# A gated linear attention kernel: state update products with 48 stationary columns in place of 64

## The chip, the cores and the metric

The kernel runs on one core of a Trainium2 chip. The metric is the device time of one execution in microseconds (us). The kernel before was timed in three runs. The trace and its page come from one further execution, taken by the hardware profiler.

The core has five engines that run their own instruction streams and wait for each other through semaphores: TensorE (matrix products, PE in the profile, with its weight loads listed apart as PEld), VectorE (DVE), ScalarE (ACT), GpSimd (POOL) and SyncE (SP), which issues the DMA transfers here. A product on TensorE has two steps: a *stationary* operand is loaded into the array (a weight load), and then a *moving* operand is streamed through it (the matmul). The result goes to PSUM, from where DVE and ACT read it.

## The reference

Two blocks follow each other. The first is a gated recurrence for 4 batches x 8 heads, 768 tokens and 48 channels per head; the second is a feed-forward block of 384 -> 2048 -> 384 with hardswish between. All is float32.

```python
state = np.zeros((B, H, D, D))                       # D = 48
for t in range(S):                                   # S = 768
    state = alpha[:, :, t, :, None] * state + np.einsum('bhd,bhe->bhde', k[:, :, t], v[:, :, t])
    y[:, :, t] = np.einsum('bhd,bhde->bhe', q[:, :, t], state)
x = y.transpose(0, 2, 1, 3).reshape(B * S, H * D)    # 3072 x 384
h = x @ w_in
out = (h * np.clip(h + 3.0, 0.0, 6.0) / 6.0) @ w_out
```

## The kernel before, in words

**The recurrence, by chunks.** The 3072 tokens are cut into 24 chunks of 128 tokens (six in each batch), and each chunk into two halves of 64. Heads go in pairs: head `a` (0 or 1) of pair `p` (0 to 3) has its 48 channels on the partitions `64*a` to `64*a + 47` of a 128-partition tile, and the 16 partitions behind them belong to no channel. A scan over the decays gives `R` (L309), and the keys are multiplied by it (L332), so that they stand in the scale of the chunk's end. The scaled keys are needed twice: by channel for the scores (L346), and by token as `kb`, for the state. For the first chunks `kb` is made by transposes on TensorE (L374) and an ACT copy (L378), for the later ones by way of a DRAM tile (`kw`, `kr`).

**The state.** For each chunk, `update` (L423 to L432; the products stand on L429) computes one 48 x 48 matrix per head and half: the half's 64 keys, by token, are the stationary operand, and the half's 64 rows of `v` are the moving one. With 4 pairs, 2 heads and 2 halves that makes 16 products, or 8 in the last chunk of a batch, where only the first half is wanted: 20 x 16 + 4 x 8 = 352 products in all. Each float32 product appears in the trace as two weight loads and two matmuls, so L429 has 704 of each. Each product uses one quarter of the array, a tile of 64 rows by 64 columns: the half `b` sets the rows, the head `a` the columns. The results lie in two PSUM banks, one for each half.

**Who uses it.** `next_state` (L435 to L440) adds these results to the state on DVE, over all 128 partitions and 192 columns at once: after the first half into `half_st` (L439 or, at a batch's start, L437), after the second into `sm`. `decayed_state` (L409, POOL) makes the next chunk's `st` of `sm`. `place_state` (L419, ACT) copies the state into rows of `v` for the product that makes the output `y` (`attend`, L455), and takes the 48 real rows of each head alone: `st[64 * a : 64 * a + D]`.

**The feed-forward block.** After the first chunks, which use plain products (L478, L489, L516), the two big products run on groups of 256 tokens with sums of blocks in place of some products (L600 for the first, L703 for the second). DVE makes the sums (L537 to L541, L647, L664), applies the hardswish (L498) and adds products; ACT copies PSUM banks out (L606) and does the first step of the hardswish (L494).

**The order.** The order of all instructions is written out by hand, as a list of words (`run(...)`, L751 to L900). `u.6.3.0` is `update` for chunk 6 with the PSUM banks 3 and 0. Each engine takes its instructions in that order, and waits on semaphores where an operand or a buffer isn't ready. No scheduler changes it.

Of the kernel before, what the change touches and what calls it, by code (L numbers as in the profile page):

```python
# [17 lines left out]
def kernel(  # L18
# [32 lines left out]
    nc = tc.nc  # L51
    B, H, S, D = q.shape
# [26 lines left out]
    half = consts.tile([C, 1], FP, tag="half")  # L79
# [141 lines left out]
    R_t, P_t, Q_t, K_t, kb_t, A_t, xT_t, ps_t = ({} for _ in range(8))  # L221
# [200 lines left out]
    def update(j, *at):  # L422
        for b, i in enumerate(at):  # L423
            ps_t["u", j, b] = banks[i][:, 0 : NP * D].rearrange("r (p n) -> r p n", p=NP)
        for p in range(NP):
            for a in range(2):
                for b in range(len(at)):
                    half = slice(HB * b, HB * b + HB)
                    nc.tensor.matmul(ps_t["u", j, b][64 * a : 64 * a + 64, p],  # L429
                                     kb_t[j][half, p, 64 * a : 64 * a + 64],  # L430
                                     v_t[j][half, b, 2 * p + a, 0:D],
                                     start=True, stop=True)  # L432

# [189 lines left out]
    def hidden1(g, o):  # L623
# [16 lines left out]
    b = {(i, k): w2[:, i * HF : (i + 1) * HF, k * HD : (k + 1) * HD]  # L640
         for i in range(2) for k in range(2)}
# [79 lines left out]
    def store2(g, i):  # L721
# [13 lines left out]
        "sc": scores, "m": masked, "qa": place_q, "kb": k_by_token, "ck": keep_k,  # L735
        "st": decayed_state, "sv": place_state, "kt": turn_k, "kw": write_k, "kr": read_k,
        "u": update, "sm": next_state, "ya": lambda j, i: attend(j, 0, i),
        "yb": lambda j: attend(j, 1), "cy": keep_x,
        "f": ff1, "fa": lambda i, m: ff1_half(0, i, m), "fb": lambda i: ff1_half(1, i, None), "fr": gate, "fg": hidden, "b": ff2, "bo": keep_out, "so": store, "x": combine_w2,
# [193 lines left out]
```

## Time and profile before

| what | value |
|---|---|
| median of 3 runs | 535.48 us (535.39 to 535.66) |
| the profiled execution: span, first to last instruction | 533.7 us |
| median less span | 1.8 us |
| granted TensorE clock over the span | 1.000 |
| PE busy / weight loads busy | 524.6 us (98%) / 499.4 us (94%) |
| DVE busy | 477.2 us (89%) |
| ACT busy / POOL busy | 257.2 us (48%) / 50.4 us (9%) |
| L429 matmuls, busy (704) | 16.8 us |
| L429 weight loads, busy (704) | 14.2 us |

The page gives the span of the profiled execution, and no total beside it; the 1.8 us by which the runs' median stands above the span is what lies around it. Busy time is a union: instructions of one engine that overlap are counted once, which is why 704 matmuls of 220 ns make only 16.8 us. In a line of groups, the shape `64*64` is rows x columns of the stationary operand, `64x48` is rows x columns of the moving one; after the bar come the busy time of the group in us and the mean length of one in ns, and then the time that the engine stood idle just before, with what ended it. The end of a matmul is modelled by the profiler, so that distances between starts say more than lengths.

### The profile page before, as it was taken

The page shows a single profiled execution, that of the slowest core. Times are in us where ns is not written, and L with a number is a line of the kernel's source. Part 1 is how long each engine was busy: PE and PEld are TensorE (multiplying, and loading weights), DVE is VectorE, ACT ScalarE, POOL GpSimd, SP SyncE. Part 2 cuts the span into 40 slices and gives each one's busy share as a digit, 9 for nine tenths or more (in the row PEclk, how much of TensorE's full clock was granted, in tenths as well). Part 3 has the DMA queues.
Part 4 walks back from the last instruction along what each step waited for, and adds up shares of the span by engine and source line. Part 5 has one row for each costly group of instructions (what it writes and reads, how often), then busy time and mean ns, then how long its engine had stood idle before and what let it go on. Part 6 is the DMA issues. An engine that isn't in the chain of part 4 may idle for free.

```text
span 533.7 us, 15143 instructions
## 1 busy us (share of the span) xinstructions
PE 524.6 (98%) x6306; PEld 499.4 (94%) x6306; DVE 477.2 (89%) x849; ACT 257.2 (48%) x503; POOL 50.4 (9%) x71
## 2 busy tenths in 40 slices
PE   8799999999999999999999999999999999999997
PEld 7698886789999999999999999999999999999997
DVE  6999989999999999998999999999999899496382
ACT  3889865212653553553544444642634544553340
POOL 5333425100000000000000000000000000000000
DMA  9998876005615155254344355044454042100001
GB/s 174 217 252 256 215 216 152 21 2 154 152 30 116 32 121 135 57 140 95 87 110 113 91 124 140 19 120 102 115 136 104 11 110 43 44 2 2 15 16 37
DMA packets 124100, 54.40 MB, mean 102 GB/s; under 512 B 83328, under 2 KB 116864, under 8 KB 124032
## 3 DMA queue, kind: packets, MB, share of 16 engines
q1 hardware_dynamic: 124032, 53.44, 42.5%
q8 instruction: 49, 0.80, 0.6%
q14 instruction: 19, 0.16, 0.1%
HBM read 44.50 MB, written 8.91 MB: 100 GB/s over the span
## 4 chain that ended last, share of the span: by engine, by line
PE 85%; DVE 8%; POOL 2%; DMA 2%; ACT 1%; issue 1%; SPq 1%; DVEq 0%; POOLq 0%
PE m_ps L703 34%; PE m_ps L600 34%; PE m_ps L478 5%; PE t_ps L455 4%; PE t_ps L346 2%; PE t_ps L429 2%; PE m_ps L489 2%; PE t_ps L282 1%; DVE rings L647 1%; DMA v<-in_v_dram 1%; DVE raw L537 1%; ACT raw L191 1%; DMA kq<-in_k_dram 1%; DVE g_sb L647 1%; DVE w L537 1%
## 5 line engine op out<-in xcount | busy, mean ns | idle before, releaser
L606 ACT COPY g_sb<-m_ps 128x512 f32<-128x512 f32 x110 | 63.6, 584 | 124.9 <-PE m_ps L600 104.1
L703 PE MATMUL m_ps<-w,g_sb 128*128 128x192 f32 x704 | 121.7, 327 | 0.0
L703 PEld LDWEIGHTS m_ps<-w,g_sb 128*128 128x128 f32 x704 | 113.7, 190 | 0.4
L703 PE MATMUL m_ps<-rings,g_sb 128*128 128x192 f32 x528 | 91.5, 326 | 0.0
L703 PEld LDWEIGHTS m_ps<-rings,g_sb 128*128 128x128 f32 x528 | 85.4, 190 | 0.1
L600 PE MATMUL m_ps<-xc,w 128*128 128x128 f32 x640 | 82.7, 277 | 0.3 <-DVE w L541 0.3
L600 PEld LDWEIGHTS m_ps<-xc,w 128*128 128x128 f32 x640 | 77.5, 192 | 1.5 <-issue 0.5
L494 ACT ACTIVATE r<-g_sb,half 128x512 f32<-128x512 f32 x80 | 56.8, 722 | 32.9 <-DVE g_sb L541 12.1
L498 DVE SCALAR_TENSOR_TENSOR g_sb<-r,g_sb 128x512 f32<-128x512 f32 x80 | 53.6, 682 | 4.6 <-ACT r L494 4.2
L600 PE MATMUL m_ps<-xT,raw 128*128 128x128 f32 x400 | 52.5, 277 | 0.0
L600 PEld LDWEIGHTS m_ps<-xT,raw 128*128 128x128 f32 x400 | 48.6, 192 | 0.6
L409 POOL TENSOR_TENSOR st<-sm,R 128x192 f32<-128x192 f32 x20 | 12.9, 643 | 353.8 <-DVE sm L439 306.7
L647 DVE TENSOR_TENSOR g_sb<-g_sb 128x512 f32<-128x512 f32 (+1 forms) x55 | 42.0, 795 | 0.2
L600 PE MATMUL m_ps<-xT,w 128*128 128x128 f32 x320 | 42.0, 276 | 0.0
L600 PEld LDWEIGHTS m_ps<-xT,w 128*128 128x128 f32 x320 | 39.3, 192 | 0.1
L366 ACT COPY A<-q 48x256 f32<-48x256 f32 x88 | 35.5, 404 | 5.0 <-DVE q L332 3.7
L356 DVE TENSOR_TENSOR A<-t_ps,mask 64x256 f32<-64x256 f32 x96 | 36.0, 414 | 0.4
L478 PE MATMUL m_ps<-xT,w 128*128 128x256 f32 x144 | 32.8, 382 | 0.0
L600 PE MATMUL m_ps<-xc,raw 128*128 128x128 f32 x240 | 31.8, 276 | 0.0
L309 DVE TENSOR_TENSOR_SCAN R<-t,ones 128x516 f32<-128x516 f32 x24 | 29.7, 1236 | 1.1 <-ACT t L300 1.0
L478 PEld LDWEIGHTS m_ps<-xT,w 128*128 128x128 f32 x144 | 26.7, 190 | 3.6
L600 PEld LDWEIGHTS m_ps<-xc,raw 128*128 128x128 f32 x240 | 29.6, 192 | 0.1
(104 smaller groups left out, 731.0 us busy)
## 6 DMA issues: line engine op xcount, KB each, us to landing
raw<-in_moe_w_out_dram SPq DMA_DIRECT2D x8, 768.0 KB, 5.2
raw<-in_moe_w_in_dram SPq DMA_DIRECT2D x6, 768.0 KB, 6.8
v<-in_v_dram SPq DMA_DIRECT2D x48, 96.0 KB, 3.0
out_dram<-oh SPq DMA_DIRECT2D x44, 96.0 KB, 1.7
far<-kq SPq DMA_DIRECT2D x64, 64.0 KB, 2.2
kb<-far SPq DMA_DIRECT2D x64, 64.0 KB, 2.0
aq<-in_alpha_dram SPq DMA_DIRECT2D x36, 96.0 KB, 2.5
qq<-in_q_dram SPq DMA_DIRECT2D x36, 96.0 KB, 2.4
```

The lines of the kernel that those rows point to most:

```text
L309: nc.vector.tensor_tensor_scan(out=reverse(R, n - 1, n), data0=reverse(ax, n, n), data1=reverse(ones, n, n), initial=0.0, op0=ALU.mult, op ...
L356: nc.vector.tensor_tensor(out=to[:, a], in0=sc[a][half], in1=mask[half, half].unsqueeze(1).to_broadcast([HB, NP, HB]), op=ALU.mult)
L366: nc.scalar.copy(out=to[:, a], in_=Q_t[j][64 * a : 64 * a + D, :, half])
L409: nc.gpsimd.tensor_tensor(out=st, in0=sm, in1=R_t[j][:, :, 0:1].to_broadcast([C, NP, D]), op=ALU.mult)
L455: nc.tensor.matmul(y_of(j, (i + 1) // 2, p)[:, HB * b : HB * b + HB], vb[:, p, e : e + 32], A_t[j][:, b, 2 * p + a], start=(b == 0 and i = ...
L478: nc.tensor.matmul(h[:, f], w1[:, kk, o : o + C], xT_t[g][:, kk], start=(kk == 0), stop=(kk == KT - 1))
L494: nc.scalar.activation(out=to, in_=h, func=AF.Relu, bias=half, scale=1.0 / 6.0)
L498: nc.vector.scalar_tensor_tensor(out=to, in0=r, scalar=1.0, in1=h, op0=ALU.min, op1=ALU.mult)
L600: nc.tensor.matmul(acc[g][i][:, f * C : (f + 1) * C], spots[w][:, f * C : (f + 1) * C], x_of(g, x), start=(first and f == 0), stop=last, s ...
L606: nc.scalar.copy(out=slots[z], in_=acc[g][i])
L647: nc.vector.tensor_tensor(out=out, in0=in0, in1=in1, op=ALU.subtract)
L703: nc.tensor.matmul(to[g], a, rhs[:, f], start=(first and f == 0), stop=(last and f == HF - 1), skip_group_check=True)
```

## The change

In the products of `update`, the stationary operand is the 48 columns of the head's channels, where it was 64 columns (48 and the 16 behind them). The output takes 48 partitions of the PSUM bank, where it took 64; the other 16 keep what the bank held before. Rows, moving operand, tile of the array (64 x 64), order of all instructions on all engines, and semaphore waits are the same. `next_state` still reads 128 partitions.

```diff
             for a in range(2):
                 for b in range(len(at)):
                     half = slice(HB * b, HB * b + HB)
-                    nc.tensor.matmul(ps_t["u", j, b][64 * a : 64 * a + 64, p],
-                                     kb_t[j][half, p, 64 * a : 64 * a + 64],
+                    nc.tensor.matmul(ps_t["u", j, b][64 * a : 64 * a + D, p],
+                                     kb_t[j][half, p, 64 * a : 64 * a + D],
                                      v_t[j][half, b, 2 * p + a, 0:D],
                                      start=True, stop=True)
```

## The prediction

> **What bounds the kernel now.** I read the page's busy times first, then the busy times by stage, then the groups of instructions by shape.
>
> ```profile
> PE 524.6 (98%) x6306; PEld 499.4 (94%) x6306; DVE 477.2 (89%) x849; ACT 257.2 (48%) x503; POOL 50.4 (9%) x71
> ```
>
> ```profile
> 0.00:60.00 60.00, 54.04 (x820) 47.75 (x821) 54.33 (x93) 47.83 (x77) 23.52 (x34) 1.00 1.00 221
> 60.00:155.00 95.00, 94.71 (x997) 81.36 (x996) 92.59 (x153) 42.03 (x81) 16.75 (x22) 1.00 0.47 117
> 155.00:466.00 311.00, 311.00 (x3908) 306.01 (x3907) 290.23 (x532) 145.54 (x306) 10.14 (x16) 1.00 0.40 94
> 466.00:533.60 67.60, 64.82 (x588) 64.31 (x586) 40.08 (x74) 21.83 (x42) 0.00 (x0) 1.00 0.05 14
> ```
>
> Columns of the second fence: stretch, its length, busy time of PE, weight loads, DVE, ACT, POOL, then clock and DMA. TensorE is the bound from 155 us to 466 us: no idle time in 311 us, while DVE has 20.8 us of it. Up to 155 us it is not the bound alone: in the first 60 us it idles for 6 us, and from 60 to 155 DVE is busy for 92.6 of 95 us. The clock is 1.00 throughout, so it isn't a term.
>
> Next, what one weight load and one matmul cost. These are the groups by shape (first loads, then matmuls):
>
> ```profile
> L600 PEld LDWEIGHTS m_ps<-xc,w 128*128 128x128 f32 x640 | 77.5, 192 | 1.5 <-issue 0.5
> L455 PEld LDWEIGHTS t_ps<-A,v 128*32 128x32 f32 x1536 | 22.4, 110 | 3.7 <-DVE s L439 0.8 <-ACT A L366 0.6 <-issue 0.3
> L429 PEld LDWEIGHTS t_ps<-v,kb 64*64 64x64 f32 x704 | 14.2, 134 | 4.0 <-issue 2.9 <-DMA v<-in_v_dram 0.2
> L346 PEld LDWEIGHTS t_ps<-q,k 48*64 48x64 f32 x768 | 13.6, 134 | 3.2 <-issue 1.3 <-DVE q L332 0.4 <-DVE raw L210 0.3
> ...
> L455 PE MATMUL t_ps<-A,v 128*32 128x64 f32 x1536 | 25.5, 220 | 0.9 <-DVE s L439 0.7 <-ACT A L366 0.2
> L429 PE MATMUL t_ps<-v,kb 64*64 64x48 f32 x704 | 16.8, 220 | 1.3 <-issue 1.2
> ```
>
> The length of a load goes with its columns: 192 ns at 128, 134 at 64, 110 at 32. Rows don't matter: 48 rows (L346) and 64 rows (L429) both take 134. Matmuls all read about 220 ns because four tiles of the array overlap, so the time per round must come from the timeline. Two updates there, the first of 16 products and the second of 8 (a batch's last chunk), weight loads only:
>
> ```profile
> 281.46 0.56 PEld L429 LDWEIGHTS t_ps<-v,kb 64*64 64x64 f32 x32
> ...
> 338.49 0.56 PEld L429 LDWEIGHTS t_ps<-v,kb 64*64 64x64 f32 x16
> ```
>
> 32 loads on four tiles and 16 loads on two tiles take the same 0.56 us. So tiles work side by side, and the time is that of one tile's 8 loads in a row: 0.56 less one length (0.135) is 0.425 us; less 0.02 for the offset of the four tiles (0.013 for two tiles, whose starts lie wider), it is 7 steps of 58 ns. An update is 8 rounds of 58 ns.
>
> **The change part by part.**
>
> *What sets a round.* Each round on a tile is a load of 64 columns and a matmul with 48 moving columns. Loads of 128 columns (L600, eight products of which start every 0.89 us, so 111 ns) against 58 at 64 columns give (111 - 58) / 64 = 0.83 ns a column and 5 ns a round that stays. For the matmul side, L455 has loads of 32 columns and 64 moving ones, in rounds of four tiles: 64 matmuls in 1.10 us (timeline at 135.88) make 16 rounds, (1.10 - 0.22 - 0.02) / 15 = 57 ns; by its own load it would be 32 x 0.83 + 5 = 32, so there the 64 moving columns set the round, at 57 ns. The update's 48 moving columns then need some 57 - 16 x 0.83 = 44 ns. So L429 is held by its load (58) and not by its matmul (44).
>
> *With 48 columns.* The load would need 58.4 - 16 x 0.83 = 45 ns, one ns above the matmul side. A round falls by 13.2 ns. Bounds: if the matmul side held at 47 ns, the gain is 11.4; if a load's length follows the tile (64 wide still) and not the columns, it is 0; on the other side, see the rival of the lost overlap. I take 13.2, since the three loads by columns (192, 134, 110) lie on a line and 48 lies between two of them.
>
> The rule of the Trainium skill says the same of the load: in "TensorE: Matmul & The Clock Gate", section "LDWEIGHTS (loading the stationary operand)", the time is the columns divided by 1.2 in ns, whatever the rows. By it the load goes from 53 to 40 ns, 13.3 less, and the sum below is the same. The rows of 134 ns for 48 and for 64 rows agree with it.
>
> *How many rounds.* 24 updates x 7 steps between rounds = 168, and some 12 updates that don't follow another step on 64-column tiles show their first load as well: 180 x 13.2 = 2.4 us if all lay on the path.
>
> *What of it is on the path.* From 155 us on there are 16 updates (464 matmuls of L429 in that stretch): 16 x 7 + 6 = 118, x 13.2 = 1.56 us. In two of them products of L346 stand between, which hides a little; I take 1.5. TensorE never idles there, so its stream is the path, and what is taken out of it stays out if DVE and ACT can follow. DVE's 20.8 us of idle time in that stretch is 14 times that, and the longest waits in the kernel are of ACT for TensorE:
>
> ```profile
> ACT g_sb L606 <- PE m_ps L600: 104.1, 61, 5.9
> ```
>
> Where DVE is the late one (by the semaphore times of the trace, some fifteen places where a product's operand is ready only 0.13 to 0.4 us ahead), the cover is thin, and if DVE did not move up there, up to 1.5 us would go; but DVE itself stands behind products of TensorE by then, and moves up with it.
>
> *Before 155 us.* Eight updates, at most 8 x 7 x 13.2 + 6 x 13.2 = 0.8 us. Here TensorE catches up with others:
>
> ```profile
> 24.90 1.27 PE L489 MATMUL m_ps<-xT,w 128*128 128x128 f32 x9 [0.25 <-POOL w L217]
> ...
> 128.04 1.13 PE L600 MATMUL m_ps<-xc,w 128*128 128x128 f32 x8 [0.29 <-DVE w L541]
> ```
>
> What an update gives is lost at the next such place, unless the engine waited for had itself waited for the update. At 128 us TensorE waits for DVE's weight sums, which do not depend on any update, and again behind ACT copies near 143 and 146 us. Between 0 and 0.8 I take 0.2: of the eight updates' savings only what comes after the last of these, or moves DVE in the first 60 us through L439 (8.2 us of waits for L429), survives.
>
> *What costs nothing.* No instruction is added or moved, no wait is added, and no DMA or queue is touched. DVE's L439 and L437 still work on 128 partitions, 0.35 us each; the 16 stale rows of each head flow through L409 and L439 and are dropped at L419. The switch to another tile shape behind an update (about 0.15 us to the next product) has no columns in it: it is the same behind L455 with 32 columns. Also what follows first from an earlier end, DVE's addition, comes 0.1 us sooner, which lies beside other work.
>
> *Sum.* 1.5 + 0.2 = 1.7 us off the span: 533.7 becomes 532.0, and with the 1.8 us around it, 535.48 - 1.7 = 533.8 us, or 0.32% less. A change of 0.2% is 1.07 us, about what a measurement of this kernel can tell from none.
>
> **The rivals.**
>
> *The load follows the tile.* Every load in this trace fills its tile's columns (128, 64, 32), so none shows whether 48 in a tile of 64 is cheaper. If the time goes with the tile, nothing changes: 535.5 us. Against it: rows do not fill their tile in L346 (48 of 64), which runs as it should, though rows cost nothing in any case. Chance 0.12.
>
> *A floor under small operands.* If loads had a floor that lets only a quarter of the 16 columns count (an assumed share), a round would be 58.4 - 4 x 0.83 = 55 ns; 3.3 ns a round gives 180 x 3.3 = 0.6 us at the most and 0.4 us on the path by the same shares: 535.1 us, within 0.2%. For it speaks that lengths do not fall in proportion (134 at 64, 110 at 32); against it, that they fall at all between 64 and 32 columns, by 24 ns, nearly 0.83 x 32 = 27. Chance 0.08. The Trainium skill has such a rule in "TensorEngine Tiling (Array Packing)", section "Instruction Overhead": about 60 cycles for each matmul, so that a small dimension isn't worth cutting. It is told of the free dimension of a matmul, and no run here shows it for a load.
>
> *The lost overlap: slower.* If a partly filled tile could no longer take its next load while its matmul runs, load and matmul would add up in each round: 40 + 40 = 80 ns against 58, 22 more. With 166 such steps that is 3.7 us, of which some 3.1 lie on the path: 538.6 us. The place is L429 alone. That the two can add up is seen where an update starts cold (after L600): its first step is longer than the others, so that 32 matmuls take 0.68 us (timeline at 259.16) and not 0.63 (at 281.52). Against it: L429, L346 and L455 all overlap in every later round, whatever their rows. It decides from 8 ns a round upwards (66 ns): from there the result is slower by over 0.2%. Chance 0.10.
>
> *All of it on the path.* If the early updates keep their share too: 535.5 - 2.4 = 533.1 us. Chance 0.03; the waits at 128 us speak against it.
>
> **How the numbers follow.** The forecast has 0.67, with a range of its own from 533.3 (the early updates keep half) to 534.2 us (11.4 ns a round, nothing early). With the case of all on the path, faster by over 0.2% has 0.70; the tile and the floor make 0.20 for within 0.2%; slower has the overlap's 0.10. The range goes from 533.0, below all on the path, to 535.6, which takes in the floor and the unchanged time, and leaves out the overlap.
>
> **What would show it.** Right: the loads of L429 in the group view shorten from 134 to about 122 ns; an update of 32 takes 0.46 us of loads at 281 us and not 0.56; L429's busy time falls from 16.8 to about 14.5 us; later instructions start earlier by steps of 0.09 us an update. Wrong: the loads stay at 134 ns and 0.56 us (the tile), or an update grows to 0.7 us and more (the overlap), or L429 shrinks while idle time of PE before L600, L703 or L455 grows by as much (DVE did not follow).

## The result, and the profile after

The changed kernel takes 533.68 us (median of 5 runs, 533.54 to 533.84), the kernel before on the same chip 535.66 us (535.39 to 535.74): 1.98 us less. The ratio is 0.9965, with a 95% interval from 0.9953 to 0.9978. The forecast was 533.8 us, 1.7 us less than the 535.48 us of the earlier runs. The span of the profiled execution goes from 533.7 to 531.8 us.

The groups of L429 and its two neighbours on TensorE, of the changed kernel, loads first:

```profile
L455 PEld LDWEIGHTS t_ps<-A,v 128*32 128x32 f32 x1536 | 22.4, 110 | 3.9 <-DVE s L439 1.1 <-issue 0.7 <-ACT A L366 0.6
L346 PEld LDWEIGHTS t_ps<-q,k 48*64 48x64 f32 x768 | 13.5, 134 | 3.3 <-issue 1.3 <-DVE q L332 0.4 <-DVE raw L210 0.3
L429 PEld LDWEIGHTS t_ps<-v,kb 64*48 64x48 f32 x704 | 11.6, 121 | 4.1 <-issue 2.9 <-DMA v<-in_v_dram 0.4
...
L429 PE MATMUL t_ps<-v,kb 64*48 64x48 f32 x704 | 14.1, 208 | 1.5 <-issue 1.0 <-DMA v<-in_v_dram 0.3 <-ACT kb L378 0.3
```

Loads of 48 columns last 121 ns and lie on the line between 110 (32 columns) and 134 (64). The number of instructions is the same. L346 and L455, which the change doesn't touch, are as before.

The same two updates as in the prediction, weight loads in the timeline of the changed kernel (start, length and count; the first has 16 products, the second 8):

```profile
280.63 0.47 PEld L429 LDWEIGHTS t_ps<-v,kb 64*48 64x48 f32 x32
...
337.35 0.46 PEld L429 LDWEIGHTS t_ps<-v,kb 64*48 64x48 f32 x16
```

0.56 us became 0.47 and 0.46. The starts give the round directly: 45 ns in nearly every step, 58 before.

Where the time left the path is seen by one and the same instruction in both timelines, the first product of L600 after the last update. Before, and then after:

```profile
464.16 0.60 PE L429 MATMUL t_ps<-v,kb 64*64 64x48 f32 x13
...
465.24 1.16 PE L600 MATMUL m_ps<-xc,w 128*128 128x128 f32 x8
```

```profile
462.42 0.51 PE L429 MATMUL t_ps<-v,kb 64*48 64x48 f32 x13
...
463.39 1.16 PE L600 MATMUL m_ps<-xc,w 128*128 128x128 f32 x8
```

TensorE stands 1.85 us earlier there, and exactly as much at its last instruction. Laying all matmuls of the two traces side by side, the lead is 0.19 us at 144 us, and from there it grows only at the 16 updates, by 0.093 to 0.107 us at nearly all of them (0.136 at one that waits in its middle): 1.66 us from these 16. Between updates it doesn't change.

The stages of the changed kernel (columns as in the prediction) say why nothing was lost:

```profile
60.00:155.00 95.00, 94.58 (x998) 81.21 (x997) 92.73 (x154) 42.25 (x81) 16.79 (x22) 1.00 0.48 117
155.00:466.00 311.00, 311.00 (x3923) 306.02 (x3922) 291.79 (x536) 146.71 (x309) 10.14 (x16) 1.00 0.42 94
466.00:531.80 65.80, 62.98 (x571) 62.47 (x570) 38.29 (x68) 20.41 (x39) 0.00 (x0) 1.00 0.05 15
```

PE has no idle time in the middle stage, with 15 more matmuls in it than before; DVE's busy time there rose from 290.23 to 291.79 us, since four more of its instructions fall into the same 311 us. Ahead of that stage it is otherwise: at 128 us, where DVE is late, the lead fell from 0.28 to 0.15 us, and TensorE's wait in the timeline grew by as much (0.29 us before). Another 0.06 us went at 143.6 us. The wait at 128 us in the changed kernel:

```profile
127.89 1.13 PE L600 MATMUL m_ps<-xc,w 128*128 128x128 f32 x8 [0.42 <-DVE w L541]
```

### The profile page after: what moved, and what is told of

Same layout as the page of the kernel before. It is cut to its first block, busy times and chain, and to the rows that moved or that the text cites. A ratio compares the mean times of both kernels' runs of the same rounds, so it can differ in the third digit from the quotient of the medians.

```text
span 531.8 us, 15143 instructions
## 1 busy us (share of the span) xinstructions
PE 522.2 (98%) x6306; PEld 496.9 (93%) x6306; DVE 477.0 (90%) x849; ACT 257.4 (48%) x503; POOL 50.4 (9%) x71
## 4 chain that ended last, share of the span: by engine, by line
PE 81%; DVE 9%; ACT 3%; DMA 3%; POOL 2%; issue 1%; SPq 0%; DVEq 0%; POOLq 0%; ACTq 0%
PE m_ps L703 34%; PE m_ps L600 34%; PE m_ps L478 4%; PE t_ps L455 3%; PE t_ps L346 2%; PE t_ps L429 2%; DMA v<-in_v_dram 1%; DMA raw<-in_moe_w_out_dram 1%; DVE rings L647 1%; DVE R L309 1%; DVE raw L537 1%; ACT raw L186 1%; DVE g_sb L647 1%; ACT raw L191 1%; DVE w L537 1%
## 5 line engine op out<-in xcount | busy, mean ns | idle before, releaser
L600 PE MATMUL m_ps<-xc,w 128*128 128x128 f32 x640 | 82.8, 277 | 0.4 <-DVE w L541 0.4
L600 PEld LDWEIGHTS m_ps<-xc,w 128*128 128x128 f32 x640 | 77.5, 192 | 1.7 <-issue 0.6
L600 PE MATMUL m_ps<-xT,raw 128*128 128x128 f32 x400 | 52.5, 277 | 0.0
L600 PEld LDWEIGHTS m_ps<-xT,raw 128*128 128x128 f32 x400 | 48.6, 192 | 0.6
L409 POOL TENSOR_TENSOR st<-sm,R 128x192 f32<-128x192 f32 x20 | 12.9, 643 | 352.2 <-DVE sm L439 305.5
L600 PE MATMUL m_ps<-xT,w 128*128 128x128 f32 x320 | 42.0, 276 | 0.0
L600 PEld LDWEIGHTS m_ps<-xT,w 128*128 128x128 f32 x320 | 39.3, 192 | 0.1
L600 PE MATMUL m_ps<-xc,raw 128*128 128x128 f32 x240 | 31.8, 276 | 0.0
L600 PEld LDWEIGHTS m_ps<-xc,raw 128*128 128x128 f32 x240 | 29.6, 192 | 0.1
```

The source lines that it names most:

```text
L409: nc.gpsimd.tensor_tensor(out=st, in0=sm, in1=R_t[j][:, :, 0:1].to_broadcast([C, NP, D]), op=ALU.mult)
L600: nc.tensor.matmul(acc[g][i][:, f * C : (f + 1) * C], spots[w][:, f * C : (f + 1) * C], x_of(g, x), start=(first and f == 0), stop=last, s ...
```

## The experiments

The theory: a round on a tile lasts as long as the longer of its load (0.83 ns a column, and 5) and its matmul (0.83 ns a moving column, and 3); what is taken out of the late updates comes off the end. The rivals are that only the load counts, that columns count by strips, that the early updates count in full, and that DVE's cover is thin.

### 40 columns

```diff
-                    nc.tensor.matmul(ps_t["u", j, b][64 * a : 64 * a + D, p],
-                                     kb_t[j][half, p, 64 * a : 64 * a + D],
+                    nc.tensor.matmul(ps_t["u", j, b][64 * a : 64 * a + 40, p],
+                                     kb_t[j][half, p, 64 * a : 64 * a + 40],
```

> 40 stationary columns in the update products; the last 8 key channels of each head are left out, so the state is incomplete. Moving operand still 48 columns. Theory (a round lasts as long as the longer of load and matmul; load 0.83 ns a column + 5, matmul about 43 to 44 ns at 48 moving columns): the load falls to 38 ns, the matmul takes over, a round goes from 45 to 43 or 44 ns, and the time stays within 0.3 us of the changed kernel (533.4 to 533.7). Rival (only the load counts): a round of 38.5 ns, 16 late updates x 8 x 6.6 = 0.85 us less, 532.8.

The last eight key channels of each head are left out, so the state is incomplete. Measured: 533.26 us against 535.62 before (ratio 0.9953, 0.9936 to 0.9970).

```profile
L429 PEld LDWEIGHTS t_ps<-v,kb 64*40 64x40 f32 x704 | 10.9, 113 | 4.0 <-issue 2.9 <-DMA v<-in_v_dram 0.3
...
L429 PE MATMUL t_ps<-v,kb 64*40 64x48 f32 x704 | 13.6, 205 | 1.4 <-issue 1.0 <-ACT kb L378 0.3 <-DMA v<-in_v_dram 0.2
```

The load got 8 ns shorter, 113 against 121 ns, but a round only 2 to 3: it takes 42 to 43 ns by the starts, and not 38. So the matmul with 48 moving columns is the floor, as the theory has it. The time is 0.14 us under its range. In the trace the late updates gain 2.00 us on the kernel before, where 1.66 us came with 48 columns. Some 112 steps with a mean of 42.4 in place of 45 ns make 0.29 us of this difference of 0.34; about the rest is in the ten rounds that start cold, behind another tile shape or a wait, where load and matmul add up (73 ns after 80).

### 56 columns

```diff
-                    nc.tensor.matmul(ps_t["u", j, b][64 * a : 64 * a + D, p],
-                                     kb_t[j][half, p, 64 * a : 64 * a + D],
+                    nc.tensor.matmul(ps_t["u", j, b][64 * a : 64 * a + 56, p],
+                                     kb_t[j][half, p, 64 * a : 64 * a + 56],
```

> 56 stationary columns in the update products. Theory (time by single columns): loads of about 128 ns, rounds of 51.7 ns, half of the gain: 0.9 to 1.0 us under the kernel before. Rival (time by strips of 16 columns, so that 48 pays and 56 doesn't): rounds of 58 ns and the time of before.

Measured: 534.81 us against 535.62 (ratio 0.9985, 0.9976 to 0.9995): 0.81 us less, a little under the expected 0.9 to 1.0. Among the runs with a granted clock of 1.000, five of ten here and fifteen of 25 of the kernel before, the medians are 534.58 and 535.53 us, 0.95 us apart.

```profile
L429 PEld LDWEIGHTS t_ps<-v,kb 64*56 64x56 f32 x704 | 13.1, 127 | 4.8 <-issue 2.9 <-DMA v<-in_v_dram 0.7 <-DVE q L332 0.3
```

Rounds take 51 or 52 ns, half way between 58 and 45, and the late updates give 0.82 us in the trace, half of 1.66. The loads of 64, 56, 48 and 40 columns last 134, 127, 121 and 113 ns: eight columns always count, so there is no strip of 16 or 32 and no floor between 40 and 64. Steps of fewer than eight columns were not tried.

### 64 moving columns

```diff
-            ps_t["u", j, b] = banks[i][:, 0 : NP * D].rearrange("r (p n) -> r p n", p=NP)
+            ps_t["u", j, b] = banks[i][:, 0 : NP * 64].rearrange("r (p n) -> r p n", p=NP)
...
-                                     v_t[j][half, b, 2 * p + a, 0:D],
+                                     v_t[j][half, b, 2 * p + a, 0:64],
...
-        u = ps_t.pop(("u", j, b))
+        u = ps_t.pop(("u", j, b))[:, :, 0:D]
```

> 48 stationary columns as in the changed kernel, but 64 moving columns (the 16 columns of v behind each head's 48 come along, and their results are not used). Theory: the load stays at 45 ns, the matmul sets the round at 56 or 57 ns, and nearly the whole gain is gone: 0 to 0.4 us under the kernel before. Rival (only the load counts): the time of the changed kernel, 1.9 us under the kernel before.

Measured: 535.46 us against 535.62 (ratio 0.9994, 0.9985 to 1.0004).

```profile
L429 PEld LDWEIGHTS t_ps<-v,kb 64*48 64x48 f32 x704 | 13.2, 120 | 4.6 <-issue 3.0 <-DMA v<-in_v_dram 0.8
...
L429 PE MATMUL t_ps<-v,kb 64*48 64x64 f32 x704 | 16.3, 219 | 2.0 <-DMA v<-in_v_dram 1.1 <-issue 1.0
```

A load is as short as in the changed kernel (120 ns), and yet the rounds are at 56 ns, and most of the gain is gone: the late updates keep 0.31 us of 1.66 in the trace, and the runs' 0.16 us can't be told from nothing. The change is worth its time because the moving side was the shorter one.

### 64 columns, 40 moving

```diff
-                    nc.tensor.matmul(ps_t["u", j, b][64 * a : 64 * a + D, p],
-                                     kb_t[j][half, p, 64 * a : 64 * a + D],
-                                     v_t[j][half, b, 2 * p + a, 0:D],
+                    nc.tensor.matmul(ps_t["u", j, b][64 * a : 64 * a + 64, p, 0:40],
+                                     kb_t[j][half, p, 64 * a : 64 * a + 64],
+                                     v_t[j][half, b, 2 * p + a, 0:40],
```

> 64 stationary columns as before, 40 moving columns in place of 48: the last 8 channels of the values are left out of the state. Theory: the load holds the round at 58 ns as before, and the time is that of the kernel before to 0.2 us, though the products have 17% fewer moving columns. Rival (the matmul side had a part in the 58 ns): rounds of about 52 ns and 0.8 us less.

The last eight channels of the values are left out of the state. Measured: 535.54 us against 535.62 (ratio 0.9995, 0.9986 to 1.0004).

```profile
282.19 0.56 PEld L429 LDWEIGHTS t_ps<-v,kb 64*64 64x64 f32 x32
```

The loads of an update still take 0.56 us and the rounds 58 ns. Before the change the load alone set the round, as the prediction read from the trace.

### The late updates alone

```diff
-                    nc.tensor.matmul(ps_t["u", j, b][64 * a : 64 * a + D, p],
-                                     kb_t[j][half, p, 64 * a : 64 * a + D],
+                    nc.tensor.matmul(ps_t["u", j, b][64 * a : 64 * a + (D if j >= 6 else 64), p],
+                                     kb_t[j][half, p, 64 * a : 64 * a + (D if j >= 6 else 64)],
```

The first six updates, up to 94 us, keep 64 columns (the text on record says 110 us, where the seventh begins). On the same chip the changed kernel ran once more:

> 48 stationary columns only in the updates of chunks 6 to 23; the first six chunks (up to about 110 us) keep 64. Theory (the late updates lie on the path, the early ones are absorbed by waits): 1.6 to 1.7 us under the kernel before, at most 0.3 us behind the changed kernel. Rival (the early updates count in full, 0.6 to 0.8 us): about 1.2 us under the kernel before.

> The changed kernel once more, on the same chip as the other two of this call. All theories: 1.7 to 2.0 us under the kernel before; a second trace shows how far the time of TensorE at 143 us varies from execution to execution.

Measured: 533.71 us with the late updates alone, 533.72 us for the changed kernel, 535.53 us before (ratios 0.9967, 0.9954 to 0.9979, and 0.9966, 0.9952 to 0.9980). The late updates alone thus gained 1.82 us, 0.1 more than the range on record and as much as the whole change. So the first six updates give nothing that can be measured; by the intervals, each of some 0.7 us to either side, a few tenths can't be excluded. The second trace of the changed kernel repeats the first: a lead of 0.20 us at 144 us and 1.83 us at the end.

### Much more out of the late updates

```diff
-        for p in range(NP):
+        for p in range(NP if j < 6 else 1):
```

> The changed kernel, and from chunk 6 on update makes the products of head pair 0 alone; those of pairs 1 to 3 are left out, so the state is wrong there. That takes 6 of 8 rounds of 45 ns out of 16 updates, 4.3 us of TensorE's time, and changes no other engine's work. Theory (DVE and ACT have room, and move up with TensorE): the whole 4.3 us comes off, 529.3 to 529.6 us. Rival (the cover is thin, DVE becomes the bound as soon as some hundred ns are gained): less than 3 us comes off, and idle time of TensorE appears between 155 and 466 us.

Measured: 529.21 us, 4.5 us under the changed kernel on the same chip and 6.3 under the kernel before (ratio to the latter 0.9881, 0.9868 to 0.9895), 0.1 us under the expected range. Its stages:

```profile
60.00:155.00 95.00, 94.08 (x951) 80.64 (x949) 92.70 (x155) 42.05 (x82) 16.79 (x21) 1.00 0.47 117
155.00:462.00 307.00, 307.00 (x3576) 301.92 (x3576) 291.28 (x536) 146.85 (x309) 10.16 (x16) 1.00 0.40 95
```

PE still has no idle time from 155 to 462 us, and its lead over the changed kernel grows there by 4.2 us, of the 4.3 that were taken out of 16 updates. The places where the prediction has an operand ready only 0.13 to 0.4 us ahead did not bind even with a lead of several us: DVE and ACT moved up with TensorE there.

The edit takes products out of 18 updates, and not of 16 as the text on record counts: chunks 6 and 7 come before 155 us. These two show the other case. The one at 109 us gains 0.27 us on the changed kernel, and at 128 us 0.33 us of lead are lost, where TensorE's wait for DVE is 0.74 us in place of 0.42. What is taken out of the one at 141 us is lost at once, behind a wait for ACT:

```profile
141.13 1.16 PE L600 MATMUL m_ps<-xT,w 128*128 128x128 f32 x8 [0.18 <-ACT g_sb L606]
```

## Why the prediction held, step by step

**What sets a round: right.** 45 ns was forecast for 48 columns, and the starts give 45; 58 to 45 is the 13.2 ns of the sum. That the load set the round before is shown by the fewer moving columns (58 still), and that the matmul side is close behind at about 44 ns by the 40 columns (42 to 43). The rule of the Trainium skill ("TensorE: Matmul & The Clock Gate", "LDWEIGHTS (loading the stationary operand)": columns divided by 1.2, in ns) agrees with steps of 6.6 to 6.7 ns for 8 columns, at 64, 56 and 48, where the load sets the round. Two readings on the way there were loose. The loads at 128, 64 and 32 columns don't lie quite on a line (0.91 ns a column above 64, 0.75 below). And matmuls don't read about 220 ns because four tiles overlap: in the update at 338 us, on two tiles, they read 218 ns as well. Neither enters the sum.

**The late updates: right, sized a little low.** 1.5 us was taken, and the traces show 1.66. The term at fault is the count. The prediction gave 16 x 7 steps, added the first load in six updates, and took 0.06 off for two updates with products of L346 between. In the trace ten updates gain eight steps or more (0.105 us and above): seven start cold, three that wait in their middle start anew there, and the two mixed ones, which are among the seven, lost nothing. So 16 x 7 + 10 = 122 steps, and two more in the one of 0.136 us, make 124 x 13.3 = 1.65 us.

**The early updates: right as far as it can be told.** 0.2 us was taken, 0.19 and 0.20 us are what the two traces of the changed kernel have at 144 us, and leaving out the first six cost nothing measurable. But a single trace is a weak witness there, see the last section: that these two agree with 0.2 is in part luck.

**What costs nothing: one error.** The prediction said that the switch to another tile shape behind an update has no columns in it, since it is the same behind L455. The two are indeed alike before the change (149 ns there, 148 behind L429), but that did not show that columns have no part in it. They have: the distance from the last matmul of L429 to the next product fell from 148 to 135 ns. That is one of the eight steps by which an update gets shorter, so the count above holds it; the prediction reached nearly the same number by counting seven steps between rounds, of which an update behind L346 gains only six. That the two errors cancel is luck.

**Who follows: right.** PE's stream is the path from 155 to 462 us, as the one pair of heads shows. The line given as the longest wait in the kernel (ACT for L600, 104.1 us) is not that: POOL's L409 waits 306.7 us for DVE. The sum doesn't rest on it.

**The time: closer than the gain.** The forecast of 533.8 us is 0.1 off, but the gain is 1.98 us (1.81 in the second measurement, 1.85 and 1.83 in the traces) where 1.7 was forecast. The kernel before took 0.18 us more in the comparison than in the runs from which the prediction started; that part of the hit is luck. The lower end of the forecast's own range, 533.3 us, is some 0.3 us lower than half of the early updates makes it (1.5 + 0.4 us off 535.48 is 533.6).

**The rivals.** A load by the tile (no change) and a floor of small operands are excluded by 121, 127 and 113 ns at 48, 56 and 40 columns. The rule on small dimensions ("TensorEngine Tiling (Array Packing)", "Instruction Overhead", of the Trainium skill) thus doesn't bear on loads here: their time falls with every eight columns at 56, 48 and 40, all below 60. The lost overlap did not come: 80 ns is seen only in first rounds that start cold, and there it was 93 before. Its price was set too high as well: 3.1 us of 3.7 on the path is more than the shares of the prediction's own sum give (1.7 of 2.4, so 2.6 us). All of the gain on the path (2.4 us) did not come either: the traces have 1.85 and 1.83 us.

## What to carry to other kernels

Where a product uses a part of the array, compare load and matmul for each tile: in this kernel the longer of the two sets the round, and padding on the longer side costs time in proportion (seen in steps of eight columns), while padding on the shorter one is free within the rounds. Read the round from equal counts on one tile (32 loads on four tiles took as long as 16 on two), and not from the lengths of the instructions, which overlap. What a small step saves off a saturated engine can come off the end in full, even when another engine is 94% busy, if that engine takes its pace from the first; in a stage that waits for others some or all of it is lost at the next wait.

## What the runs showed that was not expected

**The way out of an update costs load plus matmul.** From the start of the last load of L429 to the next product of another tile shape the traces have 191 ns at 64 stationary and 48 moving columns, 184 at 56 and 48, 178 at 48 and 48, 173 at 40 and 48, and 184 at 64 and 40. Each is 98 to 100 ns more than 0.83 times the sum of both counts; only 48 and 64 stands out, where it is 200 ns, 107 more. L455 in the kernel before, on other tiles, has 203 to 204 ns with 32 and 64, where the sum would give 178. So the sum holds where the load sets the round, or nearly does, and not where the moving side is clearly the longer. Why is not shown.

**The first 35 us vary from execution to execution.** In these profiled executions, TensorE's position against the kernel before at 34 to 45 us lies anywhere from 0.3 us ahead (40 columns) to 0.8 us behind (40 moving columns, and the late updates alone, whose runs are as fast as those of the changed kernel), while a change of one update is worth 0.1 us. The wait at 128 us changes this by less than 0.2 us. From 155 us on, two traces of one program agree to some 0.03 us. So a few tenths of a us in the early part can't be read from one trace, while 0.01 us an update can in the late part.

Two sources of this can be seen. With the late updates alone, TensorE falls back by nearly 1 us in the third update, at 33 us, where it waits, among other things, 0.27 us for rows of `v` by DMA. And in the executions with 56 columns and with 40 moving ones the granted clock was 0.83 and 0.87 from 18 to 24 us, and 0.94 and 0.91 from there to 35 us, where it was 1.00 in the others. Products that the change doesn't touch took longer there; before, and then with 56 columns:

```profile
22.11 1.10 PE L455 MATMUL t_ps<-A,v 128*32 128x64 f32 x64 [0.69 <-DVE s L439]
```

```profile
21.96 1.94 PE L455 MATMUL t_ps<-A,v 128*32 128x64 f32 x64 [0.47 <-DVE s L439]
```

TensorE lost 0.63 and 0.67 us there, in these two executions, and at 155 us it still stood 0.47 and 0.78 us behind the kernel before.
